# A layer 1 gate step whose operations are put in another order

## The chip, the cores and the metric

One core of a Trainium2 chip runs the whole program. Its engines are TensorE (PE; its weight loads are shown as PEld), VectorE (DVE), ScalarE (ACT), GpSimd (POOL) and SyncE (SP, which here issues transfers). Each engine takes its own instructions in the order in which the program issues them and waits where an instruction needs another engine's result. The metric is the time of one execution on the device in microseconds, as a median of several runs. The kernel before takes 1412.36 us (three runs, 1409.13 to 1415.45).

## The reference

The reference is an attention with pooled queries, followed by two feed-forward layers:

```python
q_pool = q.reshape(B, H, S // 2, 2, D).mean(axis=3)          # 4, 8, 576, 64
attn   = softmax(q_pool @ k^T / sqrt(D))                     # k: 4, 8, 1152, 64
x      = (attn @ v).transpose(0, 2, 1, 3).reshape(2304, 512)
h = x @ w1_in;  g = h - tanh(h);              x = g @ w1_out # 512 -> 2048 -> 512
h = x @ w2_in;  g = h * sigmoid(1.702 * h);   x = g @ w2_out # 512 -> 2048 -> 512
```

The weights arrive as 64-bit floats, the rest as 32-bit floats.

## The kernel before, in words

To keep accuracy, every operand of a matmul is held as a high part (rounded to the format that TensorE multiplies) and a low part (what the rounding left), and three products are added up: high by high, high by low, low by high. A high part is a copy on ScalarE; a low part is a subtraction, `value - high`, on GpSimd or VectorE with both inputs in SBUF.

The attention comes first and isn't touched. The two feed-forward layers are in `moe`. Tokens are cut into 6 blocks of 384 (`b`), the hidden width of 2048 into 4 quarters of 512 (`qq`), and each quarter into two halves (`fp`). A step is one (layer, quarter, block, half): steps 0 to 47 are layer 1, steps 48 to 95 layer 2, and 12 steps make a quarter. In step w TensorE computes h of step w (L552, 24 matmuls into one of two PSUM buffers) and then y of step w-2 (L627, 24 matmuls in layer 1), which lies in four PSUM banks. Even steps begin a sum in these banks and odd steps end it, so in odd steps the four banks are added to `xb` in SBUF (L640 on VectorE; in a layer's first quarter L638, a copy on ScalarE), and the even step behind begins its sum in a bank when the bank has been read.

`gate` makes g from h. In layer 1 that is a polynomial where |h| is small, and h - tanh(h) elsewhere. On ScalarE: u = h squared (L577), a and e, squares of u plus a constant (L580, L589), d = tanh(h) (L587), and a mask from u, written over a (L594). On VectorE: g = GC * u * h (L581), which reads h in PSUM; g = (a + GA1) * g (L584); d = h - d (L592), which reads h in PSUM; g = (e + GB1) * g (L595); and a predicated copy of d into g under the mask (L598). u, a, e and d have one buffer each, g has two. `split_g` of the step before stands in this step: the high part is L562 on ScalarE, the low part L564 on GpSimd in layer 1.

Weights of the next quarter are loaded and converted in eight pieces a quarter. A piece is a load (L109, two buffers), a first conversion step s0 (L122 on ScalarE; L123 and L127 on VectorE), a second one s1 (L134 and L138 on VectorE), and the split into high (L145, ScalarE) and low part (L146, GpSimd). A table gives for each of them a slot; there are two slots a step, one ahead of it and one behind it, so before the change these jobs never stand inside `gate`. The low parts of x for the next blocks or the next layer (L102, VectorE) are put into such slots too.

The order on every engine is the order of the program text (`tc.manual_schedule`); semaphores are added where one engine needs another.

Of the kernel before, what the change touches and what calls it, by code (L numbers as in the profile page):

```python
# [10 lines left out]
AF = mybir.ActivationFunctionType  # L11
ALU = mybir.AluOpType
# [6 lines left out]
GC = 0.006269319676  # L19
GA0, GA1 = 0.64716092, 2.51604723 ** 2  # L20
# [3 lines left out]
def f32(ap):  # L24
    return ap.bitcast(F32)
# [3 lines left out]
def tile_pooled_attention_two_moe(  # L29
# [11 lines left out]
    nc = tc.nc  # L41
# [9 lines left out]
    NB = NT // TB  # L51
    NKC = DM // 128
    DFF = w1_in.shape[0] * 128
    NQ = DFF // 512
# [43 lines left out]
    def split_x(b, cs, eng):  # L98
        for c in cs:
            hi, lo = xs[b][0][c], xs[b][1][c]  # L100
            nc.scalar.activation(hi, xb[b][:, c], AF.Copy)
            eng.tensor_tensor(lo, xb[b][:, c], f32(hi), op=ALU.subtract)  # L102
# [53 lines left out]
    def weight(kind, n):  # L156
        return slots[kind][n % NSLOT[kind]]
# [369 lines left out]
    def moe(ctx: ExitStack, ending):  # L527
        mp = ctx.enter_context(tc.tile_pool(name="moe", bufs=1))
        ps_h = ctx.enter_context(tc.tile_pool(name="ps_h", bufs=2, space=PSUM))
        ps_y = ctx.enter_context(tc.tile_pool(name="ps_y", bufs=4, space=PSUM))  # L530
        add_slot("o", mp.tile([128, 2 * DM], F32R, name="w3"))
        for b in range(1, NB):
            t = mp.tile([128, 2, NKC, TB], F32R, name=f"hl{b}")
            xs[b] = [[t[:, r, c] for c in range(NKC)] for r in range(2)]

        jobs = [(li, qq, b) for li in range(2) for qq in range(NQ) for b in range(NB)]
        steps = [(*j, fp) for j in jobs for fp in range(2)]
        gg, gs, yt = {}, {}, {}

        def temp(nm, bufs=1):  # L540
            return mp.tile([128, 2, TB], F32, tag=nm, name=nm, bufs=bufs)

        def h_part(n):
            li, qq, b, fp = steps[n]
            x = xs[b]
            hb = ps_h.tile([128, 2, 512], F32, tag="h", name="h")
            for j in range(2):
                wi = weight("i", li * NQ * 4 + qq * 4 + 2 * fp + j)
                k = 0
                for c in range(NKC):  # L550
                    for w, r in ((0, 0), (0, 1), (1, 0)):
                        nc.tensor.matmul(  # L552
                            hb[:, j, 0:TB], wi[:, c, w, :], x[r][c],
                            start=(k == 0), stop=(k == 3 * NKC - 1))
                        k += 1
            return hb[:, :, 0:TB]

        def split_g(n):
            li = steps[n][0]
            gt = mp.tile([128, 2, 2, TB], F32R, tag="g", name="g", bufs=3)  # L560
            g = gg.pop(n)
            nc.scalar.activation(gt[:, :, 0, :], g, AF.Copy)  # L562
            eng = nc.gpsimd if li == 0 else nc.vector
            eng.tensor_tensor(gt[:, :, 1, :], g, f32(gt[:, :, 0, :]), op=ALU.subtract)  # L564
            gs[n] = gt

        def gate(n, h, adds):

            g = temp("gg", 2)

            def add(scalar=False):
                if adds and adds[0][0] is scalar:
                    adds.pop(0)[1]()

            if steps[n][0] == 0:
                u, a, e, d = temp("u"), temp("a"), temp("e"), temp("d")
                nc.scalar.activation(u, h, AF.Square)  # L577
                if n > 0:
                    split_g(n - 1)
                nc.scalar.activation(a, u, AF.Square, bias=GA0)  # L580
                nc.vector.scalar_tensor_tensor(  # L581
                    out=g, in0=u, scalar=GC, in1=h, op0=ALU.mult, op1=ALU.mult)
                add()
                nc.vector.scalar_tensor_tensor(  # L584
                    out=g, in0=a, scalar=GA1, in1=g, op0=ALU.add, op1=ALU.mult)
                add(True)
                nc.scalar.activation(d, h, AF.Tanh)  # L587
                add(True)
                nc.scalar.activation(e, u, AF.Square, bias=GB0)  # L589
                add(True)  # L590
                add()
                nc.vector.tensor_sub(d, h, d)  # L592
                add()
                nc.scalar.activation(a, u, AF.Relu, bias=-T2)  # L594
                nc.vector.scalar_tensor_tensor(  # L595
                    out=g, in0=e, scalar=GB1, in1=g, op0=ALU.add, op1=ALU.mult)
                add()
                nc.vector.copy_predicated(g, a[:].bitcast(I32), d)  # L598
            else:
                split_g(n - 1)  # L600
                s = temp("a")
                nc.scalar.activation(s, h, AF.Sigmoid, scale=1.702)  # L602
                add()
                nc.vector.tensor_mul(g, h, s)
            gg[n] = g
            while adds:
                adds.pop(0)[1]()

        def y_part(n):
            li, qq, b, fp = steps[n]  # L610
            g = gs.pop(n)
            base = li * NQ * 4 + qq * 4 + 2 * fp
            nm, w = (NKC, TB) if li == 0 else (NTT, DM)
            if fp == 0:
                yt[li, qq, b] = [
                    ps_y.tile([128, 512], F32, tag="y", name="y") for _ in range(nm)]
            ys = yt[li, qq, b]
            for m in range(nm):
                k = 0
                for j in range(2):  # L620
                    wo = weight("o", base + j)
                    for p, r in ((0, 0), (0, 1), (1, 0)):
                        if li == 0:
                            lhsT, rhs = wo[:, p, m * 128:(m + 1) * 128], g[:, j, r, :]
                        else:
                            lhsT, rhs = g[:, j, p, m * 128:(m + 1) * 128], wo[:, r, :]
                        nc.tensor.matmul(  # L627
                            ys[m][:, 0:w], lhsT, rhs,
                            start=(fp == 0 and k == 0), stop=(fp == 1 and k == 5))
                        k += 1  # L630
            if fp == 0:
                return []
            acc = flat(xb[b])

            def add(m):
                dst = acc[:, m * w:(m + 1) * w]
                if qq == 0:
                    nc.scalar.activation(dst, ys[m][:, 0:w], AF.Copy)  # L638
                else:
                    nc.vector.tensor_add(dst, dst, ys[m][:, 0:w])  # L640
                if li == 1 and qq == NQ - 1:
                    r0 = b * TB + m * 128
                    nc.sync.dma_start(out=out[r0:r0 + 128, :], in_=dst)

            return [(qq == 0, lambda m=m: add(m)) for m in range(nm)]

        later = {}

        def at(slot, job):
            later.setdefault(slot, []).append(job)  # L650

        for slot, job in zip((2, 4, 8, 1, 1, 3), ending):
            at(slot, job)
        per = 4 * NB
        for qn in range(1, 2 * NQ):
            for kind, f, *when in (
# [3 lines left out]
            ):  # L660
                for job, o in zip(piece(kind, qn * 4 + f), when):
                    at((qn - 1) * per + o, job)
        for b in range(1, NB):
            for c in range(NKC):
                at(4 * b - 6 + c if b > 1 else 0, lambda b=b, c=c: split_x(b, [c], nc.vector))
        for b in range(NB):
            for c in range(NKC):
                at(NQ * per - 14 + 4 * b + 2 * c, lambda b=b, c=c: split_x(b, [c], nc.vector))

        for w in range(len(steps) + YLAG):  # L670
            if w == len(steps):
                split_g(w - 1)
            for go in later.pop(2 * w, ()):
                go()
            h = h_part(w) if w < len(steps) else None
            adds = y_part(w - YLAG) if w >= YLAG else []
            if h is not None:
                gate(w, h, adds)
            while adds:
                adds.pop(0)[1]()  # L680
            for go in later.pop(2 * w + 1, ()):
                go()
        assert not later

    with tc.manual_schedule():
        with ExitStack() as c1:
            ending = attention(c1)
# [46 lines left out]
```

## Time and profile before

| | before |
|---|---|
| median of 3 runs | 1412.36 us |
| profiled execution | 1410.96 us |
| its span, first to last instruction | 1409.2 us |
| mean granted TensorE clock | 0.983 |
| busy share of the span: PE, PEld, DVE, ACT, POOL | 94%, 88%, 78%, 60%, 32% |
| layer 1's first L581 to its last | 558.6 to 997.4 us |

The profile's times count from the span's first instruction. A row of a group of instructions has the line, the engine, the operation, the tiles (output, then inputs) with their shapes, the count, the busy time and the mean length of one, then the engine's idle time just before them and which engine and line ended most of it. A row of a timeline has the start, the length and the same names; what stands in brackets is the idle time before it and what ended that. Records of neighbouring instructions on one engine can overlap by about 0.1 us, since one is still writing when the next begins.

### The profile page before, as it was taken

To read this page: it belongs to the slowest core of one execution; us is meant where nothing else is said; L and a number is where in the kernel's file an instruction comes from. 1 tells how busy PE (TensorE), PEld (TensorE's weight loads), DVE (VectorE), ACT (ScalarE), POOL (GpSimd) and SP (SyncE) were. 2 spreads that over 40 slices of the span, in tenths; PEclk is the share of its full clock that TensorE was granted. 3 is DMA by queue.
4 is the path that set the end of the run, shared out by engine and by line. 5 is a ranking of instruction groups with operands and counts; after the bars stand their busy time and mean duration, and the time that the engine had idled before them with its cause. 6 is when DMAs were issued, how large, how long until landed. Compare 5 with 4: busy or idle time off the path is not lost.

```text
span 1409.2 us, 20874 instructions
## 1 busy us (share of the span) xinstructions
PE 1319.7 (94%) x7632; PEld 1246.7 (88%) x7632; DVE 1097.9 (78%) x1230; ACT 842.4 (60%) x1885; POOL 446.2 (32%) x314
## 2 busy tenths in 40 slices
PE   4999999999999888989999999988999999999998
PEld 3999989998989887889988988988999999999997
DVE  5888888889898978999999999999963454554433
ACT  2788888888888776676655555655643332222211
POOL 6344445444545435333332332332210110110000
PEclk9999999999999999999999999999999999999999
DMA  7576666575656542110111111111011110110011
GB/s 192 131 172 162 172 143 148 140 178 144 164 144 180 116 112 64 48 36 31 45 46 30 40 36 45 31 45 46 31 46 45 45 46 30 45 46 30 24 45 67
DMA packets 44039, 117.72 MB, mean 84 GB/s; under 512 B 11936, under 2 KB 11936, under 8 KB 43936
## 3 DMA queue, kind: packets, MB, share of 16 engines
q1 hardware_dynamic: 43900, 116.38, 31.3%
q8 instruction: 60, 0.98, 0.3%
q14 instruction: 43, 0.35, 0.1%
q10 hardware_dynamic: 36, 0.00, 0.0%
HBM read 66.58 MB, written 4.79 MB: 51 GB/s over the span
## 4 chain that ended last, share of the span: by engine, by line
PE 51%; DVE 25%; issue 8%; ACT 8%; DMA 4%; POOL 3%; SPq 2%; DVEq 0%; POOLq 0%; ACTq 0%
PE y L627 17%; PE h L552 16%; PE pv L348 9%; DVE wt L134 4%; PE mx L281 4%; DVE gg L584 3%; PE sc L319 3%; PE sc L320 3%; DVE gg L595 3%; DVE gg L598 2%; DVE gg L581 2%; DVE mt L284 2%; DVE wt L127 2%; ACT ph L323 2%; ACT pf L321 1%
## 5 line engine op out<-in xcount | busy, mean ns | idle before, releaser
L321 ACT ACTIVATE pf<-sc 128x288 f32<-128x288 f32 x576 | 244.6, 426 | 70.5 <-PE sc L320 67.1
L323 ACT ACTIVATE ph<-sc 128x288 fp32r<-128x288 f32 x564 | 243.8, 432 | 0.0
L284 DVE TENSOR_REDUCE mt<-mx 128x1 fp32r<-128x1152 f32 x144 | 194.0, 1349 | 55.7 <-PE mx L281 55.7
L332 DVE TENSOR_TENSOR pl<-pf,ph 128x576 fp32r<-128x576 f32 x224 | 208.4, 952 | 6.9 <-ACT ph L323 6.4
L319 PE MATMUL sc<-q,a 128*128 128x288 f32 x576 | 169.3, 305 | 10.2 <-ACT ph L323 4.1
L320 PE MATMUL sc<-q,a 65*128 65x288 f32 x576 | 167.1, 302 | 2.0 <-DMA q<-tt 2.0
L602 ACT ACTIVATE a<-h 128x768 f32<-128x768 f32 x48 | 39.0, 813 | 208.1 <-PE h L552 208.1
L640 DVE TENSOR_TENSOR xb<-xb,y 128x384 f32<-128x384 f32 (+1 forms) x126 | 76.0, 605 | 95.1 <-PE y L627 95.1
L348 PE MATMUL pv<-pl,vh 128*128 128x288 f32 x576 | 139.5, 306 | 10.6 <-POOL pl L332 7.1
L564 POOL TENSOR_TENSOR g<-gg,g 128x768 fp32r<-128x768 f32 x48 | 93.5, 1947 | 171.6 <-ACT g L562 168.5
L552 PE MATMUL h<-hl,w 128*128 128x384 f32 x720 | 134.1, 341 | 7.4 <-DVE hl L102 7.4
L348 PE MATMUL pv<-ph,vh 128*128 128x288 f32 x576 | 136.9, 301 | 3.9 <-ACT u L354 3.8
L552 PEld LDWEIGHTS h<-hl,w 128*128 128x128 f32 x720 | 128.8, 192 | 9.2 <-DVE hl L102 8.0
L562 ACT ACTIVATE g<-gg 128x768 fp32r<-128x768 f32 x96 | 81.2, 846 | 90.8 <-DVE gg L598 51.4
L348 PE MATMUL pv<-ph,vl 128*128 128x288 f32 x576 | 135.1, 298 | 0.0
L281 PE MATMUL mx<-kh,bdq 128*128 128x384 f32 x432 | 108.4, 362 | 26.2 <-DVE mt L284 18.7
L319 PEld LDWEIGHTS sc<-q,a 128*128 128x128 f32 x576 | 112.1, 195 | 17.6 <-ACT ph L323 11.1
L332 POOL TENSOR_TENSOR pl<-pf,ph 128x576 fp32r<-128x576 f32 x64 | 106.7, 1668 | 62.3 <-ACT ph L323 53.6
L320 PEld LDWEIGHTS sc<-q,a 65*128 65x128 f32 x576 | 111.4, 193 | 2.3 <-issue 2.2
L348 PEld LDWEIGHTS pv<-pl,vh 128*128 128x128 f32 x576 | 96.9, 191 | 16.2 <-POOL pl L332 9.4
L552 PE MATMUL h<-hl,bdq 128*128 128x384 f32 x600 | 108.4, 335 | 1.2 <-DVE d L592 1.2
L348 PEld LDWEIGHTS pv<-ph,vh 128*128 128x128 f32 x576 | 102.6, 192 | 6.8 <-ACT u L354 6.6
(114 smaller groups left out, 2910.1 us busy)
## 6 DMA issues: line engine op xcount, KB each, us to landing
a<-kh SPq DMA_DIRECT2D x64, 288.0 KB
raw<-in_moe_w_in_dram SPq DMA_DIRECT2D x32, 512.0 KB
raw<-in_moe_w_out_dram SPq DMA_DIRECT2D x32, 512.0 KB
qr<-in_q_dram SPq DMA_DIRECT2D x16, 576.0 KB
kr<-in_k_dram SPq DMA_DIRECT2D x16, 576.0 KB
vr<-in_v_dram SPq DMA_DIRECT2D x16, 576.0 KB
q<-qh SPq DMA_DIRECT2D x64, 144.0 KB
a<-kl SPq DMA_DIRECT2D x32, 288.0 KB
```

The source lines that it names most:

```text
L281: nc.tensor.matmul(mx[:, a, 0:384], bdqs[p % 2][:, j, :], d["kh"][:, a * 384:(a + 1) * 384], start=True, stop=True)
L284: nc.vector.tensor_reduce(d["mt"][:, j:j + 1], mx[:, :, 0:384], AX.XY, ALU.max, negate=True)
L319: nc.tensor.matmul(sc, a1[:, ks], q2[:, xs], start=True, stop=False)
L320: nc.tensor.matmul(sc, a2[:, ks], q3[:, xs], start=False, stop=True)
L321: nc.scalar.activation(pf[:, xs], sc, AF.Exp, scale=SCALE)
L323: nc.scalar.activation(ph[:, xs], sc, AF.Exp, scale=SCALE)
L332: eng.tensor_tensor(pl, pf, f32(ph[:]), op=ALU.subtract)
L348: nc.tensor.matmul(accs[hd][x], w[:, t, :], r[:, x * HB:(x + 1) * HB], start=(t == 0 and n == 0), stop=(t == KT - 1 and n == 2))
L552: nc.tensor.matmul(hb[:, j, 0:TB], wi[:, c, w, :], x[r][c], start=(k == 0), stop=(k == 3 * NKC - 1))
L562: nc.scalar.activation(gt[:, :, 0, :], g, AF.Copy)
L564: eng.tensor_tensor(gt[:, :, 1, :], g, f32(gt[:, :, 0, :]), op=ALU.subtract)
L627: nc.tensor.matmul(ys[m][:, 0:w], lhsT, rhs, start=(fp == 0 and k == 0), stop=(fp == 1 and k == 5))
```

## The change

In layer 1's `gate`, Tanh is issued right behind Square, and VectorE's L581 behind both; the split of the step before comes next, then one addition of y, the subtraction h - d, the other additions, and only then the operations on a, e and g and the predicated copy. The weights' jobs are no longer put into slots ahead of and behind a step but at named places: "split" and "convert" inside `gate`, "start" and "end" around the step. Both conversion steps of a piece now stand at one "convert" place, and the table of steps is new. The splits of x and the last jobs of the attention's end move to such places as well. What is computed stays the same.

```diff
--- before.py
+++ after.py
@@ -564,6 +564,15 @@
             eng.tensor_tensor(gt[:, :, 1, :], g, f32(gt[:, :, 0, :]), op=ALU.subtract)
             gs[n] = gt
 
+        later = {}
+
+        def at(w, place, job):
+            later.setdefault((w, place), []).append(job)
+
+        def run(w, place):
+            for go in later.pop((w, place), ()):
+                go()
+
         def gate(n, h, adds):
 
             g = temp("gg", 2)
@@ -575,33 +584,36 @@
             if steps[n][0] == 0:
                 u, a, e, d = temp("u"), temp("a"), temp("e"), temp("d")
                 nc.scalar.activation(u, h, AF.Square)
+                nc.scalar.activation(d, h, AF.Tanh)
+                nc.vector.scalar_tensor_tensor(
+                    out=g, in0=u, scalar=GC, in1=h, op0=ALU.mult, op1=ALU.mult)
                 if n > 0:
                     split_g(n - 1)
+                run(n, "split")
+                add()
+                nc.vector.tensor_sub(d, h, d)
+                add()
+                add()
+                add()
+                run(n, "convert")
                 nc.scalar.activation(a, u, AF.Square, bias=GA0)
-                nc.vector.scalar_tensor_tensor(
-                    out=g, in0=u, scalar=GC, in1=h, op0=ALU.mult, op1=ALU.mult)
-                add()
-                nc.vector.scalar_tensor_tensor(
-                    out=g, in0=a, scalar=GA1, in1=g, op0=ALU.add, op1=ALU.mult)
-                add(True)
-                nc.scalar.activation(d, h, AF.Tanh)
                 add(True)
                 nc.scalar.activation(e, u, AF.Square, bias=GB0)
                 add(True)
-                add()
-                nc.vector.tensor_sub(d, h, d)
-                add()
+                nc.vector.scalar_tensor_tensor(
+                    out=g, in0=a, scalar=GA1, in1=g, op0=ALU.add, op1=ALU.mult)
                 nc.scalar.activation(a, u, AF.Relu, bias=-T2)
                 nc.vector.scalar_tensor_tensor(
                     out=g, in0=e, scalar=GB1, in1=g, op0=ALU.add, op1=ALU.mult)
-                add()
                 nc.vector.copy_predicated(g, a[:].bitcast(I32), d)
             else:
                 split_g(n - 1)
                 s = temp("a")
                 nc.scalar.activation(s, h, AF.Sigmoid, scale=1.702)
+                run(n, "split")
                 add()
                 nc.vector.tensor_mul(g, h, s)
+                run(n, "convert")
             gg[n] = g
             while adds:
                 adds.pop(0)[1]()
@@ -644,42 +656,38 @@
 
             return [(qq == 0, lambda m=m: add(m)) for m in range(nm)]
 
-        later = {}
-
-        def at(slot, job):
-            later.setdefault(slot, []).append(job)
-
-        for slot, job in zip((2, 4, 8, 1, 1, 3), ending):
-            at(slot, job)
-        per = 4 * NB
+        for (w, place), job in zip(
+                ((0, "end"), (1, "end"), (3, "end"), (0, "convert"), (0, "convert"), (1, "split")),
+                ending):
+            at(w, place, job)
+        places = ("end", "convert", "convert", "split")
         for qn in range(1, 2 * NQ):
             for kind, f, *when in (
-                ("i", 0, 1, 5, 5, 7), ("o", 1, 3, 7, 8, 9), ("i", 1, 5, 9, 9, 11),
-                ("o", 0, 8, 13, 13, 15), ("i", 2, 10, 15, 16, 21), ("i", 3, 13, 17, 17, 23),
-                ("o", 2, 17, 23, 24, 25), ("o", 3, 19, 25, 27, 29),
+                ("i", 0, 0, 2, 2, 3), ("o", 1, 1, 3, 3, 5), ("i", 1, 2, 4, 4, 5),
+                ("o", 0, 3, 6, 6, 7), ("i", 2, 4, 8, 8, 11), ("i", 3, 6, 10, 10, 11),
+                ("o", 2, 8, 12, 12, 13), ("o", 3, 10, 13, 13, 14),
             ):
-                for job, o in zip(piece(kind, qn * 4 + f), when):
-                    at((qn - 1) * per + o, job)
-        for b in range(1, NB):
-            for c in range(NKC):
-                at(4 * b - 6 + c if b > 1 else 0, lambda b=b, c=c: split_x(b, [c], nc.vector))
+                for job, w, place in zip(piece(kind, qn * 4 + f), when, places):
+                    at((qn - 1) * 2 * NB + w, place, job)
         for b in range(NB):
             for c in range(NKC):
-                at(NQ * per - 14 + 4 * b + 2 * c, lambda b=b, c=c: split_x(b, [c], nc.vector))
+                if b > 0:
+                    at(max(0, 2 * b - 4 + c // 2), "end" if b > 1 else "start",
+                       lambda b=b, c=c: split_x(b, [c], nc.vector))
+                at(NQ * 2 * NB - 7 + 2 * b + c, "end",
+                   lambda b=b, c=c: split_x(b, [c], nc.vector))
 
         for w in range(len(steps) + YLAG):
             if w == len(steps):
                 split_g(w - 1)
-            for go in later.pop(2 * w, ()):
-                go()
+            run(w, "start")
             h = h_part(w) if w < len(steps) else None
             adds = y_part(w - YLAG) if w >= YLAG else []
             if h is not None:
                 gate(w, h, adds)
             while adds:
                 adds.pop(0)[1]()
-            for go in later.pop(2 * w + 1, ()):
-                go()
+            run(w, "end")
         assert not later
 
     with tc.manual_schedule():
```

## Rows read from the trace of the kernel before

**Rows 1.** Busy time by stretch: us, then PE, PEld, DVE, ACT, POOL, clock, DMA.

```profile
558.61:671.04 112.43, 101.70 (x548) 100.09 (x548) 105.97 (x113) 77.30 (x124) 37.56 (x19) 0.94 0.12 36
...
782.67:894.38 111.71, 104.78 (x578) 100.83 (x577) 107.22 (x118) 63.79 (x88) 36.12 (x20) 0.98 0.12 38
...
1010.00:1409.20 399.20, 395.39 (x1998) 359.44 (x1996) 197.21 (x265) 119.55 (x174) 33.75 (x26) 1.00 0.14 44
```

**Rows 2.** Chain that ended last, 645 to 690: start, length, what.

```profile
662.85 4.16 PE h L552 x24
667.01 4.16 PE y L627 x24
```

**Rows 3.** Waits of PE, 553 to 1010: total us, times, longest.

```profile
PE y L627 <- DVE xb L640: 20.1, 13, 3.5
```

**Rows 4.** Groups on DVE, 782.7 to 894.3: count, busy us, mean ns, idle.

```profile
L134 DVE SCALAR_TENSOR_TENSOR wt<-wa,wt 128x512 f32<-128x512 f32 x8 | 16.5, 2061 | 0.7
L584 DVE SCALAR_TENSOR_TENSOR gg<-a,gg 128x768 f32<-128x768 f32 x12 | 15.4, 1285 | 2.6 <-ACT a L580 2.2
L595 DVE SCALAR_TENSOR_TENSOR gg<-e,gg 128x768 f32<-128x768 f32 x12 | 15.3, 1278 | 0.0
L598 DVE COPY_PREDICATED gg<-a,d 128x768 f32<-128x768 int32 x12 | 14.7, 1222 | 0.6
...
L127 DVE SCALAR_TENSOR_TENSOR wt<-raw,wt 128x512 int32<-128x512 int32 x8 | 7.5, 938 | 0.3
```

**Rows 5.** Timeline, 861 to 870: start, length, instruction.

```profile
861.54 0.95 DVE L595 SCALAR_TENSOR_TENSOR gg<-e,gg 128x768 f32<-128x768 f32 x1
...
862.47 0.80 ACT L577 ACTIVATE u<-h 128x768 f32<-128x768 f32 x1
862.59 1.08 DVE L598 COPY_PREDICATED gg<-a,d 128x768 f32<-128x768 int32 x1
...
863.56 0.41 DVE L123 TENSOR_SCALAR wt<-raw 128x512 int32<-128x512 int32 x1
863.76 0.85 ACT L562 ACTIVATE g<-gg 128x768 fp32r<-128x768 f32 x1 [0.50 <-DVE gg L598]
864.00 0.69 DVE L127 SCALAR_TENSOR_TENSOR wt<-raw,wt 128x512 int32<-128x512 int32 x1
...
864.69 1.84 POOL L564 TENSOR_TENSOR g<-gg,g 128x768 fp32r<-128x768 f32 x1 [7.14 <-ACT g L562]
864.80 2.28 DVE L134 SCALAR_TENSOR_TENSOR wt<-wa,wt 128x512 f32<-128x512 f32 x1
...
867.72 0.95 DVE L581 SCALAR_TENSOR_TENSOR gg<-u,h 128x768 f32<-128x768 f32 x1
...
868.59 0.55 DVE L640 TENSOR_TENSOR xb<-xb,y 128x384 f32<-128x384 f32 x1
868.71 0.81 ACT L587 ACTIVATE d<-h 128x768 f32<-128x768 f32 x1 [3.36 <-DVE gg L581]
869.05 0.95 DVE L584 SCALAR_TENSOR_TENSOR gg<-a,gg 128x768 f32<-128x768 f32 x1
869.41 0.84 ACT L589 ACTIVATE e<-u 128x768 f32<-128x768 f32 x1
```

**Rows 6.** Line L592: count, ns shortest/median/longest, first and last start.

```profile
L592 DVE TENSOR_TENSOR d<-h,d x48: 943/951/955, 560.5 to 1000.6; 128x768 f32<-128x768 f32 x48
```

**Rows 7.** Line L587: what ended ScalarE's idle time before it, us, times.

```profile
  DVE gg L581: 105.5, 34
```

**Rows 8.** Timeline, layer 2, 1020 to 1023.

```profile
1020.82 1.30 POOL L146 TENSOR_TENSOR vh<-wt,vh 128x512 fp32r<-128x512 f32 x1 [9.30 <-ACT vh L145]
1021.13 1.27 DVE L123 TENSOR_SCALAR wt<-raw 128x512 int32<-128x512 int32 x1
```

**Rows 9.** Groups on DVE, 558.7 to 671.0.

```profile
L102 DVE TENSOR_TENSOR hl<-xb,hl 128x384 fp32r<-128x384 f32 x16 | 10.8, 702 | 0.2 <-ACT hl L101 0.2
```

**Rows 10.** Chain that ended last, 979 to 1010.

```profile
984.21 5.99 PE y L627 x24
```

## The prediction

> **What bounds the kernel now.** I read the page's forty slices first (behind the attention VectorE is nearly full and TensorE just under it, then the other way round), then the busy time by stage. In two quarters of layer 1 VectorE is busy 94 and 96% and TensorE 90 and 94%; in layer 2 TensorE is busy 99% and VectorE 49% [rows 1]. So a change to the layer 1 step can move layer 1 only. Layer 1 has 48 steps; the windows are cut where the first VectorE operation of steps 0, 12, 24 and 36 begins (L581), so twelve steps take 112.4, 111.6 (from 671.04 to 782.67, the gap between two windows) and 111.7 us, 9.3 us a step. In the few stretches where TensorE works without a pause, a block of 24 matmuls of h or of y takes 4.16 us [rows 2]: 8.32 us a step, 99.8 us for twelve. TensorE's longest waits in layer 1 are for VectorE's additions of y [rows 3]. VectorE's queue therefore sets the pace and TensorE is the floor under it, 12 us a quarter lower.
>
> Why VectorE takes 9.3 us: in the third quarter, taking 0.69 us as the undisturbed length of the conversion's L127 and L134, 0.95 of L584 and L595 and 1.07 of L598, the five means give 8x1.37 + 8x0.25 + 12x0.335 + 12x0.33 + 12x0.15 = 22.7 us of lengthening [rows 4]. The cause is in the timeline: GpSimd's low part (L564) runs from 864.69 to 866.53; L134, begun at 864.80, ends at 867.08, 0.55 after GpSimd [rows 5]. An operation that reads PSUM never shows this: L592 is 943 to 955 ns in all 48 steps [rows 6]. So operations with two SBUF inputs stand still while GpSimd reads, and PSUM readers don't; that is what the change plays on. If all 22.7 us went, VectorE's queue would need 89 us a quarter and TensorE would be the bound.
>
> **The change, part by part.** (a) *Tanh moves ahead of VectorE's first operation.* Today Tanh (L587) waits for L581 in 34 of the 48 steps, 105.5 us in all [rows 7], though both only read h: at 868.71 Tanh begins 0.04 us after L581's end, while h had been there for over 6 us (Square had begun to read it at 862.47) [rows 5]. Readers of one h on two engines take turns in program order. After the change Tanh is issued first, so L581 waits for Tanh. And Tanh writes d, of which there is one buffer, read last by the copy_predicated (L598) of the step before. So a new chain stands in each step: L598's end, 0.09 to ScalarE (863.67 to 863.76), Tanh 0.81, 0.04 back: 0.94 us in which VectorE has nothing queued that may run (conversions, which filled this place, now stand later in the step). Against today's pitch, where the next operation starts 0.11 us before L598's recorded end (862.59 + 1.08 to 863.56), it costs 1.05 us a step, 12.6 us a quarter. Square isn't in the chain: it comes after Relu and ends before L598 does.
>
> The Trainium skill, "PSUM — Partial Sum Buffer", section "PSUM bank collisions raise a hardware error", says that ScalarE and VectorE may not touch one bank at once, reads included, and that a dependency is put between such instructions. The trace agrees (0.04 us behind L581). By this rule a quarter comes out as below; without it the gap would be gone and TensorE's 99.8 us would hold.
>
> (b) *What is left of the port stalls.* I count a step from L598's end to the next L598's end. L581 starts at 0.94. The copy g (L562, 0.85) follows Tanh at ScalarE's pitch of 0.70, from 0.79 to 1.64; GpSimd starts 0.08 later (864.61 to 864.69): low part from 1.72 to 3.56. A weight's low part (L146, 1.30 [rows 8]) queues behind it, to 4.88, a second one later still.
>
> Even step with a conversion: L581 0.94, L592 1.81 (pitch 0.87, as L581 to L640 [rows 5]), then the conversion's L123 at 2.68. Does a tensor_scalar with one SBUF input stand still? In layer 2 it did: begun at 1021.13 under L146, it took 1.27 us and ended 0.28 after it [rows 8]. So L123 ends at 3.84 in place of 3.09, 0.75 lost. The conversion needs 2.57 (863.56 to 867.72 less L134's 1.59 of stall), so L584 starts at 6.0, L595 at 7.05 and L598 at 8.1 (an operation that needs the one before follows 1.05 later, 861.54 to 862.59 [rows 5]), end 9.16.
>
> Odd step with y's additions: 0.94, addition 1.81, L592 2.27, additions at 3.14, 3.60, 4.06 (0.46 apart, 868.59 to 869.05), L584 4.52, L595 5.57, L598 6.62, end 7.7. Here GpSimd is hidden to 4.52; one L146 sticks out by 0.2 (7.9). With two, L584 and L595 each lose a turn: 8.9. Odd with conversion and one L146: 7.7 + 2.57 + 0.2 = 10.5. Even with conversion and L146: 9.16 + 1.1 = 10.3.
>
> The new table gives, in a quarter, five even conversion steps, one of 10.3, two of 10.5 (offsets 1 and 3: two of the eight conversions do fall into steps with additions), two of 8.9, one of 7.9, one of 7.7: 45.8 + 10.3 + 21.0 + 17.8 + 7.9 + 7.7 = **110.5 us**, against 111.6 and 111.7. Check from the other side: 111.7 - 22.7 + 12.6 + 8.7 (stalls left: 3.75 + 1.9 + 0.66 + 2.4) + 2.2 (six odd steps whose last three operations now follow one another directly) - 2.2 (L584's waits for ScalarE's a [rows 4], which go) = 110.3. The stalls fall by 14 us and the Tanh gap takes 12.6 of them.
>
> (c) *First quarter.* Additions are on ScalarE. In an odd step L584 is then ready at 2.68 and ends some 0.8 behind GpSimd at 4.4 (0.55 for 512 elements [rows 5], so about 0.8 for 768: an estimate), and Relu, behind ScalarE's additions, lets L598 begin near 6.1: 7.2, with one L146 7.6 to 7.9, with two 8.6. Sixteen low parts of x (L102, today 10.8 us on VectorE [rows 9]) now come two at the ends of steps 0 to 7 and 0.47 us each run just in the Tanh gap, at no cost; if that cover were gone, 7.5 us. Steps 0 to 11: 8.2 (0.7 for Tanh and a conversion step without a low part, 7.5), 7.6, 9.2, 10.3, 9.2, 8.6, 9.2, 7.9, 9.2, 7.2, 9.2, 8.6, and an estimated 1.5 for the normalisation behind steps 0 and 3: 105.9 against 112.4, -6.5.
>
> (d) *Last quarter.* Steps 36 to 44 are 110.5 less 7.7, 9.2 and 8.9 = 84.7; y of step 44 then starts 1.56 later (L581, addition, start), at 86.3. Today it starts at 984.21 [rows 10], 89.8 after 894.38: -3.5, because the low parts of x for layer 2 also fall into gaps. That block takes 5.99 us as its four banks come free one by one; the earlier additions let it run at about 4.16, less 0.4 for its successor's wait: -1.4. From there TensorE runs without a pause today.
>
> (e) *At nothing.* Loads: a raw buffer comes free earlier in a step and is wanted earlier in a later one, by about as much; SP's queue holds only these loads there, so nothing waits behind one. Layer 2's moved conversions: VectorE is half idle [rows 1]; if they delayed an addition by their 2.57 us, TensorE has a 4.16 us block of h in between. y of step w waits for its low part at 3.56 in step w+1 and is done 4.16 later, 5.5 us before the last addition of step w+2 wants it, so TensorE isn't late anywhere.
>
> Sum: -6.5 - 1.2 - 1.2 - 3.5 - 1.4 = -13.8 us on the profiled execution's 1410.96 (span 1409.2): 1397. That run is 1.4 under the median 1412.36; I forecast **1399**.
>
> **Bounds.** The gap's price: nothing if the turns aren't taken, 12.6 + 9.6 us a quarter if Square (0.80) came into it because h is late. I take 12.6, for all its parts have rows. Stalls left: from 0 to today's 22.7; I take 8.7, the count by the new table.
>
> **Rivals.** 1. *No gap:* Tanh of a step is free to run beside L598. A quarter of VectorE is then 97.9, TensorE's 99.8 bounds, and 45 steps at 8.32 reach y of step 44 some 47 us earlier: 1364. Against it: 34 turns taken, and one d. 7%.
> 2. *The stalls stay* (slower): in even steps only 0.96 of GpSimd's 1.84 us lies beside PSUM readers; if GpSimd is later than 1.72, or takes the port back between the five conversion operations, each L564 and L146 again blocks one operation, on top of the gap. It decides from 8.7 + 13.8/3.75 = 12.4 us of stalls a quarter; with all of today's the time is 1450, halfway (15.7) 1423. For it: L127 and L134 lose 13 us a quarter today; against it: half of the conversions then meet no L146. 15%.
> 3. *A wash:* gap 0.2 to 0.35 us longer by semaphores or a late Square, 9 to 16 us in 45 steps: 1406 to 1413. 23%. The forecast has 55%; its own range is 1385 to 1405.
>
> 0.5% (7 us) is about what a measurement of this kernel can tell from no change. Faster beyond it: 0.61; within: 0.23; slower: 0.16. The range 1382 to 1420 leaves out most of rival 1 and the far part of rival 2.
>
> **What would show it.** (a) VectorE idle about 0.9 us before each L581, released by Tanh, and Tanh released by L598; if L581 follows L598 directly, (a) is wrong. (b) L584, L595 and L598 at their undisturbed 0.95 and 1.07, L134 at 0.69, and L123 near 1.2 in even steps; stalls near 9 us a quarter. Quarters near 106, 110.5, 110.5. The forecast is wrong if the gap is absent, or if L127 and L134 keep means over 0.9.

## The result, and the profile after

The changed kernel takes 1396.32 us (median of 4 runs, 1390.82 to 1398.61) against 1413.24 us for the kernel before in the same comparison (4 runs, 1409.13 to 1415.45): ratio 0.988, 95% interval 0.984 to 0.992. The forecast was 1399. The profiled execution took 1398.61 us, its span 1396.8 us against 1409.2.

Busy time by stretch of the kernel after, cut like [rows 1] at the first VectorE operation of steps 0, 12, 24 and 36 (columns as there):

```profile
562.08:665.66 103.58, 98.63 (x547) 96.55 (x547) 94.36 (x109) 75.20 (x122) 33.68 (x18) 0.97 0.14 44
665.66:775.18 109.52, 105.15 (x586) 102.52 (x585) 94.42 (x113) 66.17 (x93) 34.11 (x20) 0.98 0.13 39
775.18:884.84 109.66, 103.62 (x578) 99.50 (x577) 94.56 (x116) 64.77 (x89) 33.85 (x20) 1.00 0.12 39
```

The quarters took 112.4, 111.6 and 111.7 us and now take 103.6, 109.5 and 109.7. VectorE is busy 86% of the third quarter, where it was 96%, and yet the quarter is only 2 us shorter. The timeline at the beginning of step 24, an even step with a conversion, shows why (ScalarE's and GpSimd's rows stand between VectorE's; TensorE's are left out):

```profile
773.15 1.09 DVE L608 COPY_PREDICATED gg<-a,d 128x768 f32<-128x768 int32 x1
774.27 0.81 ACT L587 ACTIVATE d<-h 128x768 f32<-128x768 f32 x1 [1.46 <-DVE gg L608]
774.98 0.84 ACT L562 ACTIVATE g<-gg 128x768 fp32r<-128x768 f32 x1
775.18 0.95 DVE L588 SCALAR_TENSOR_TENSOR gg<-u,h 128x768 f32<-128x768 f32 x1 [0.94 <-ACT d L587]
...
775.89 1.86 POOL L564 TENSOR_TENSOR g<-gg,g 128x768 fp32r<-128x768 f32 x1 [3.66 <-ACT g L562]
776.05 0.95 DVE L594 TENSOR_TENSOR d<-h,d 128x768 f32<-128x768 f32 x1
...
776.91 1.12 DVE L123 TENSOR_SCALAR wt<-raw 128x512 int32<-128x512 int32 x1
...
778.07 0.69 DVE L127 SCALAR_TENSOR_TENSOR wt<-raw,wt 128x512 int32<-128x512 int32 x1
778.87 0.69 DVE L134 SCALAR_TENSOR_TENSOR wt<-wa,wt 128x512 f32<-128x512 f32 x1
...
782.32 1.08 DVE L608 COPY_PREDICATED gg<-a,d 128x768 f32<-128x768 int32 x1
```

(L588 is the first operation, before L581; L594 the subtraction, before L592; L603, L606 and L608 were L584, L595 and L598; the additions are L652.) Tanh begins 0.03 us after the predicated copy ends, the first operation 0.10 after Tanh, and VectorE stands idle for 0.94 us. GpSimd's low part, 775.89 to 777.75, runs beside the subtraction, which reads h in PSUM, at no cost; L123 meets its end and takes 1.12 in place of 0.41; L134, which took 2.28 beside GpSimd in [rows 5], takes 0.69. From copy end to copy end the step takes 9.16 us (774.24 to 783.40).

VectorE's groups over the third quarter, answering to [rows 4] (count, busy us, mean ns, idle time before):

```profile
L606 DVE SCALAR_TENSOR_TENSOR gg<-e,gg 128x768 f32<-128x768 f32 x12 | 13.3, 1110 | 1.3
L608 DVE COPY_PREDICATED gg<-a,d 128x768 f32<-128x768 int32 x12 | 12.9, 1077 | 1.2
...
L603 DVE SCALAR_TENSOR_TENSOR gg<-a,gg 128x768 f32<-128x768 f32 x12 | 11.7, 975 | 0.0
L588 DVE SCALAR_TENSOR_TENSOR gg<-u,h 128x768 f32<-128x768 f32 x12 | 11.4, 954 | 11.2 <-ACT d L587 11.2
...
L123 DVE TENSOR_SCALAR wt<-raw 128x512 int32<-128x512 int32 x8 | 7.7, 964 | 0.0
L127 DVE SCALAR_TENSOR_TENSOR wt<-raw,wt 128x512 int32<-128x512 int32 x8 | 6.5, 813 | 0.3
L134 DVE SCALAR_TENSOR_TENSOR wt<-wa,wt 128x512 f32<-128x512 f32 x8 | 5.5, 692 | 0.8
```

The lengthening is 8x0.55 (L123) + 8x0.12 (L127) + 12x0.15 (L606) + 0.4 (L603, L608) = 7.6 us, where it was 22.7. In exchange L588 has 11.2 us of idle time before it, all ended by Tanh. Over the whole layer it waits for Tanh in 34 of 48 steps; at the layer's beginning and end x's low parts (L102) fill the gap.

Where the 12.4 us of the two spans lie: the first h begins at 556.2 in place of 553.4, 2.8 later, in the attention, which the change doesn't touch (over the ten profiled kernels of this study, all with the same attention, the first VectorE operation of layer 1 starts anywhere from 555.1 to 565.1). From there to y of step 44 it is 415.3 us against 430.8, -15.5; to the first h of layer 2 -1.3; over layer 2's first quarter +1.7; the rest is equal.

### The profile page after: what moved, and what is told of

It reads as the page before. It is cut to its first block, busy times and chain, and to the rows that moved or that the text cites. A ratio compares the mean times of both kernels' runs of the same rounds, so it can differ in the third digit from the quotient of the medians.

```text
span 1396.8 us, 20802 instructions
## 1 busy us (share of the span) xinstructions
PE 1316.1 (94%) x7632; PEld 1243.2 (89%) x7632; DVE 1048.5 (75%) x1230; ACT 843.7 (60%) x1885; POOL 439.5 (31%) x314
## 4 chain that ended last, share of the span: by engine, by line
PE 47%; DVE 28%; ACT 9%; issue 5%; DMA 4%; POOL 3%; SPq 3%; DVEq 0%; POOLq 0%; ACTq 0%
PE y L639 14%; PE h L552 14%; PE pv L348 9%; PE mx L281 4%; DVE gg L606 3%; DVE gg L603 3%; PE sc L319 3%; DVE gg L608 3%; PE sc L320 3%; DVE d L594 3%; DMA vr<-in_v_dram 2%; ACT d L587 2%; DVE wt L123 2%; DVE wt L127 2%; DVE gg L588 2%
## 5 line engine op out<-in xcount | busy, mean ns | idle before, releaser
L564 POOL TENSOR_TENSOR g<-gg,g 128x768 fp32r<-128x768 f32 x48 | 89.0, 1853 | 300.3 <-ACT g L562 281.0
L652 DVE TENSOR_TENSOR xb<-xb,y 128x384 f32<-128x384 f32 (+1 forms) x126 | 73.0, 606 | 93.2 <-PE y L639 93.2
L281 PE MATMUL mx<-kh,bdq 128*128 128x384 f32 x432 | 108.4, 362 | 24.4 <-DVE mt L284 16.8
L552 PE MATMUL h<-hl,w 128*128 128x384 f32 x720 | 130.5, 335 | 0.0
L605 ACT ACTIVATE a<-u 128x768 f32<-128x768 f32 x48 | 40.7, 848 | 131.8 <-DVE gg L603 131.8
L320 PEld LDWEIGHTS sc<-q,a 65*128 65x128 f32 x576 | 111.6, 194 | 3.1 <-issue 3.1
L615 DVE TENSOR_TENSOR gg<-h,a 128x768 f32<-128x768 f32 x48 | 45.8, 955 | 84.8 <-ACT a L612 84.8
L348 PEld LDWEIGHTS pv<-ph,vh 128*128 128x128 f32 x576 | 102.5, 192 | 7.1 <-ACT u L354 6.9
```

The source lines that it names most:

```text
L281: nc.tensor.matmul(mx[:, a, 0:384], bdqs[p % 2][:, j, :], d["kh"][:, a * 384:(a + 1) * 384], start=True, stop=True)
L320: nc.tensor.matmul(sc, a2[:, ks], q3[:, xs], start=False, stop=True)
L348: nc.tensor.matmul(accs[hd][x], w[:, t, :], r[:, x * HB:(x + 1) * HB], start=(t == 0 and n == 0), stop=(t == KT - 1 and n == 2))
L552: nc.tensor.matmul(hb[:, j, 0:TB], wi[:, c, w, :], x[r][c], start=(k == 0), stop=(k == 3 * NKC - 1))
```

## The experiments

My theory: the change takes 14 us of stalls behind GpSimd out of a quarter and puts a Tanh gap of 12.6 us in. Against it stood that the gap isn't what it seems, that the stalls fall for other reasons, and that the order and the new places don't share the gain as I thought. Every time below is a median, each ratio is against the kernel before in the same comparison.

**1. Take the gap away by d's buffer.** d and e take turns in two shared buffers, so that Tanh needn't wait for the copy.

```diff
-                u, a, e, d = temp("u"), temp("a"), temp("e"), temp("d")
+                u, a = temp("u"), temp("a")
+                first, second = temp("de", 2), temp("de", 2)
+                d, e = (first, second) if n % 2 == 0 else (second, first)
```

> The changed kernel with one edit: d and e share two buffers and change places every step, so Tanh of a step writes where e of the step before lay, and waits for that step's L606 (g = (e + GB1) * g) and no more for its predicated copy. Theory (the gap of 0.94 us before each first VectorE operation is the chain copy, Tanh, first operation through the one buffer of d): Tanh then starts when Square is done, about 0.6 us before the copy's end; the gap shrinks to about 0.25 us, an even step with a conversion from 9.16 to about 8.5 us, a quarter from 109.6 to about 101.3 us; with TensorE's floor of 99.8 near, 1365 to 1375 us. Rival (the first operation is late for another reason, h's arrival or Square's): gap and time stay, 1396 us. Second rival (the stalls come back as GpSimd's low part falls on other operations): gap gone, the mean of the conversion's operations up by 0.6 us each, time 1385 to 1396 us.

Measured: 1373.25 us, ratio 0.974 (0.971 to 0.977). The second and third quarters take 102.5 and 102.2 us. VectorE's rows around the start of step 34, then ScalarE's, then a group of the third quarter:

```profile
848.12 1.08 DVE L610 COPY_PREDICATED gg<-a,de 128x768 f32<-128x768 int32 x1
849.47 0.95 DVE L590 SCALAR_TENSOR_TENSOR gg<-u,h 128x768 f32<-128x768 f32 x1 [0.27 <-ACT de L589]
```

```profile
847.87 0.81 ACT L588 ACTIVATE u<-h 128x768 f32<-128x768 f32 x1
848.58 0.81 ACT L589 ACTIVATE de<-h 128x768 f32<-128x768 f32 x1
```

```profile
L123 DVE TENSOR_SCALAR wt<-raw 128x512 int32<-128x512 int32 x8 | 8.8, 1101 | 0.0
```

Tanh (here L589) now follows Square directly and ends 0.19 us behind the copy; the gap is 0.27 us. It is the chain through d that cost the changed kernel some 20 us (0.014 of the ratio; 23 between medians of two comparisons). This version beats both kernels; with that of experiment 2, from which the ratios don't tell it apart, it is the fastest found that computes the whole.

**2. Take the gap away by the turns.** d keeps one buffer; Tanh goes back behind the first operation and the subtraction behind the additions.

```diff
-                nc.scalar.activation(d, h, AF.Tanh)
                 nc.vector.scalar_tensor_tensor(
                     out=g, in0=u, scalar=GC, in1=h, op0=ALU.mult, op1=ALU.mult)
                 if n > 0:
                     split_g(n - 1)
+                nc.scalar.activation(d, h, AF.Tanh)
                 run(n, "split")
                 add()
-                nc.vector.tensor_sub(d, h, d)
                 add()
                 add()
                 add()
+                nc.vector.tensor_sub(d, h, d)
```

> The changed kernel with Tanh issued behind VectorE's first operation (as before the change) and the subtraction h - d behind all four additions; d keeps its one buffer. Theory (the gap needs Tanh's turn on h ahead of the first operation as well as d's one buffer, so taking either away ends it): the first operation follows the predicated copy at once, Tanh runs beside the additions in odd steps; in even steps the subtraction waits for Tanh until about 1.75 us behind the copy, which puts the conversion's L123 near GpSimd's end and leaves it 0.1 us of stall in place of 0.75; an even step with a conversion 8.5 us, a plain odd step 6.7 us, a quarter about 101.5 us; 1368 to 1378 us. Rival (the 0.94 us only move from ahead of the first operation to ahead of the subtraction): a quarter 108 us or more, 1388 to 1396 us.

Measured: 1377.35 us, ratio 0.972 (0.969 to 0.975); a quarter takes 101.8 us, an even step with a conversion 8.5, the plain odd one 6.67. VectorE's groups in the third quarter:

```profile
L597 DVE TENSOR_TENSOR d<-h,d 128x768 f32<-128x768 f32 x12 | 11.5, 958 | 5.3 <-ACT d L591 5.3
L587 DVE SCALAR_TENSOR_TENSOR gg<-u,h 128x768 f32<-128x768 f32 x12 | 11.3, 943 | 0.0
```

The wait for Tanh has moved ahead of the subtraction but is 5.3 us a quarter and no longer 11.2: 0.88 us in each of the six even steps, none in the odd ones, where the additions cover it. So the gap before the first operation needs both: Tanh's turn on h first, and d's one buffer.

**3. Take the port stalls away.** In the kernel before, and in the changed one, GpSimd's low part of g in layer 1 is left out: a memset writes zeros to the same tile and reads nothing.

```diff
-            eng.tensor_tensor(gt[:, :, 1, :], g, f32(gt[:, :, 0, :]), op=ALU.subtract)
+            if li == 0:
+                nc.gpsimd.memset(f32(gt[:, :, 1, :]), 0.0)
+            else:
+                eng.tensor_tensor(gt[:, :, 1, :], g, f32(gt[:, :, 0, :]), op=ALU.subtract)
```

For the kernel before:

> The kernel before, in which GpSimd's low part of g in layer 1 (L564) is a memset to zero: the low part of g is left out, so the output lacks it; GpSimd still writes the tile but reads nothing. Theory (two-input VectorE operations stand still because GpSimd reads SBUF): L134, L584 and L595 fall to 0.69 and 0.95 us but for the weights' low parts, the lengthening from 22.7 to about 6 us a quarter, and TensorE bounds: 1365 to 1380 us. Rival (they stand still for something else at that place, such as ScalarE's copy into the same tile or a semaphore): the means stay, 1410 us.

For the changed kernel:

> The changed kernel, in which GpSimd's low part of g in layer 1 (L564) is a memset to zero: the low part of g is left out. Theory (of the stalls left in a quarter, 7.6 us by the trace, all but those behind the weights' low parts fall, while the Tanh gap of 0.94 us stays in every step): a quarter 103 to 105 us, 1370 to 1380 us, and VectorE still idle about 0.9 us before each first operation. Rival (the gap is itself due to GpSimd): the gap goes too, TensorE bounds at 99.8 us, 1358 us as the kernel before with the same edit.

Measured: the kernel before falls to 1358.08 us (0.963, 0.960 to 0.967), below the 1365 to 1380 that I expected, and its third quarter takes 99.8 us, in which TensorE is busy throughout (columns as in [rows 1]):

```profile
754.60:854.40 99.80, 99.80 (x577) 99.80 (x576) 92.92 (x117) 62.98 (x89) 21.78 (x20) 1.00 0.13 43
```

The changed kernel falls to 1371.1 us only (0.971, 0.969 to 0.973), with 103.5 us a quarter. VectorE's groups, third quarter, first of the former:

```profile
L587 DVE SCALAR_TENSOR_TENSOR gg<-a,gg 128x768 f32<-128x768 f32 x12 | 11.5, 957 | 2.3 <-ACT a L583 1.9
...
L134 DVE SCALAR_TENSOR_TENSOR wt<-wa,wt 128x512 f32<-128x512 f32 x8 | 5.5, 690 | 0.7
```

and of the latter:

```profile
L591 DVE SCALAR_TENSOR_TENSOR gg<-u,h 128x768 f32<-128x768 f32 x12 | 11.5, 954 | 10.6 <-ACT d L590 10.6
...
L123 DVE TENSOR_SCALAR wt<-raw 128x512 int32<-128x512 int32 x8 | 4.9, 619 | 0.0
```

L134's mean goes from 2061 to 690 ns and L584's (here L587) from 1285 to 957 once GpSimd reads nothing there. That alone doesn't prove it, since the memset needn't wait for ScalarE and mostly runs elsewhere in the step. Rows that do lie beside a memset settle it: in layer 1 of the changed kernel eight L609 (L595 before the change) begin while one runs, and each takes its undisturbed 0.96 us. So for operations with two SBUF inputs the stalls are due to GpSimd's reads; L123 is another matter (last section). The stalls behind the weights' low parts stay in both kernels. The Tanh gap stays (10.6 us), so it isn't GpSimd's. With the reads of g gone the kernel before is the faster of the two, by 13 us between the medians of two comparisons (0.963 against 0.971).

**4. The order alone, and the places alone.** First the kernel before with the new order of `gate` and the old slots:

```diff
                 nc.scalar.activation(u, h, AF.Square)
+                nc.scalar.activation(d, h, AF.Tanh)
+                nc.vector.scalar_tensor_tensor(
+                    out=g, in0=u, scalar=GC, in1=h, op0=ALU.mult, op1=ALU.mult)
                 if n > 0:
                     split_g(n - 1)
...
```

> The kernel before with the order of gate alone changed (Tanh and the first operation first, then the split, the subtraction, additions, and the rest); conversions and splits keep their slots ahead of and behind the steps. Theory (the order brings the gain, the new places give half of it back because they leave the Tanh gap empty): conversions in their slots fill the gap; a quarter 100 to 104 us, 1363 to 1382 us, faster than the whole change's 1396 us. Rival (the gain comes from keeping the conversions off GpSimd's low parts of weights, that is from the new places): 1396 to 1413 us, and the stalls of L127 and L134 as before the change, near 13 us a quarter.

Measured: 1406.89 us, ratio 0.998 (0.996 to 1.000). My theory was wrong here. VectorE's groups of its third quarter:

```profile
L134 DVE SCALAR_TENSOR_TENSOR wt<-wa,wt 128x512 f32<-128x512 f32 x8 | 13.2, 1648 | 0.7
...
L579 DVE SCALAR_TENSOR_TENSOR gg<-u,h 128x768 f32<-128x768 f32 x12 | 11.4, 947 | 2.8 <-ACT d L578 2.8
L127 DVE SCALAR_TENSOR_TENSOR wt<-raw,wt 128x512 int32<-128x512 int32 x8 | 11.3, 1419 | 0.3
L138 DVE SCALAR_TENSOR_TENSOR wt<-raw,wt 128x512 int32<-128x512 int32 x9 | 9.3, 1030 | 0.3
```

The conversions do fill the gap (2.8 us of it left), but there L127, L134 and L138 meet GpSimd's low parts, of weights and of g, and lose 5.8 + 7.7 + 3.0 = 16.5 us a quarter, more than the 13 us of before the change. With the operations on g that is some 18 us of lengthening against 22.7, and the 2.8 us of gap take most of the difference.

Then the changed kernel with the old order of `gate`, the split place behind the split of g and the convert place behind the subtraction (shown against the order before the change):

```diff
                 if n > 0:
                     split_g(n - 1)
+                run(n, "split")
                 nc.scalar.activation(a, u, AF.Square, bias=GA0)
...
                 nc.vector.tensor_sub(d, h, d)
                 add()
+                run(n, "convert")
                 nc.scalar.activation(a, u, AF.Relu, bias=-T2)
```

> The changed kernel with the old order of gate: first operation, then a and L584's turn, Tanh behind the first operation, the subtraction, then the new convert place, then the rest; the new split place stands behind the split of g. Theory by the durations of the trace (no Tanh gap, as Tanh follows the first operation; but L584 now meets GpSimd's low part of g in every step and loses 1.1 to 1.9 us, while the conversions run free behind it): an even step with a conversion 9.2 us, plain odd steps 7.8 us, a quarter about 107 us; 1385 to 1393 us, that is the new places bring all of the gain and the order none. Rival (the order of VectorE's operations is what gains): 1405 us or above, near the order's own -3 us away from before.

Measured: 1389.93 us, ratio 0.985 (0.983 to 0.986), not to be told apart from the whole change's 0.988 (0.984 to 0.992). The theory held in the time. The price stands in VectorE's groups again:

```profile
L594 DVE SCALAR_TENSOR_TENSOR gg<-a,gg 128x768 f32<-128x768 f32 x12 | 19.6, 1632 | 11.9 <-ACT a L590 11.9
```

L584 (here L594) waits 11.9 us a quarter for a and stands still 8.1 us behind GpSimd; the conversions run free (L134 at 692 ns). In a step that is 1.67 us, within the 1.1 to 1.9 of the expectation, but the larger part is a wait for ScalarE, which the expectation didn't name. So the new places bring the gain. The new order trades L584's wait and stall for Tanh's gap and L123's stall, about one for one.

**5. Fill the gap with conversions.** Both conversion steps of a piece stand behind the step before that of their convert place.

```diff
-        places = ("end", "convert", "convert", "split")
+        places = ("end", "end", "end", "split")
...
-                for job, w, place in zip(piece(kind, qn * 4 + f), when, places):
-                    at((qn - 1) * 2 * NB + w, place, job)
+                for j, (job, w, place) in enumerate(zip(piece(kind, qn * 4 + f), when, places)):
+                    at((qn - 1) * 2 * NB + w - (j in (1, 2)), place, job)
```

> The changed kernel with one edit: both conversion steps of a piece stand behind the step before the one whose convert place they had, so that VectorE runs them between a predicated copy and the next first operation. Theory (VectorE is idle there and the conversion's tensor_scalar stands still 0.75 us behind GpSimd only because it comes at 2.68 us): the 2.57 us of a conversion fill the gap, the next first operation starts at about 2.5 in place of 0.94 us, L123's stall is gone; an even step takes about 7.3 us in place of 9.16, a quarter 97 to 101 us with TensorE's 99.8 as the floor; 1360 to 1370 us. Rival (conversions must stand in steps without additions, after the subtraction, or GpSimd's low parts block them again): L127 to L138 grow to means of 1.2 us and more, time 1396 us or above.

Measured: 1392.09 us, ratio 0.987 (0.985 to 0.990), a third quarter of 108.5 us: a miss by over 20 us. The timeline shows what the expectation had left out:

```profile
806.40 1.08 DVE L608 COPY_PREDICATED gg<-a,d 128x768 f32<-128x768 int32 x1
...
809.14 1.87 POOL L564 TENSOR_TENSOR g<-gg,g 128x768 fp32r<-128x768 f32 x1 [7.24 <-ACT g L562]
809.34 2.22 DVE L138 SCALAR_TENSOR_TENSOR wt<-raw,wt 128x512 int32<-128x512 int32 x1
```

and the group that it is so in the whole quarter (each of them takes 2.21 to 2.23 us):

```profile
L138 DVE SCALAR_TENSOR_TENSOR wt<-raw,wt 128x512 int32<-128x512 int32 x9 | 20.0, 2222 | 0.3
```

GpSimd started 1.66 us behind the copy, L138 at 1.86, and every conversion lost 1.53 us for 0.2 us. The expectation asked only what becomes of L123; by the 1.72 us at which the prediction itself had GpSimd begin, the last operation of the conversion came too late as well. The gap was filled (3.7 us of idle time left in the quarter), L123's stall was gone, and one new stall took nearly all of it.

**6. Push L123 past GpSimd, on top of experiment 1.** Two of the four additions go to the end of the step, behind the copy.

```diff
                 nc.vector.tensor_sub(d, h, d)
                 add()
-                add()
-                add()
                 run(n, "convert")
```

> The kernel in which d and e share two buffers, with two of the four additions of y left to the end of the odd step, behind the predicated copy, where they read PSUM while GpSimd makes the low part of the next step. Theory (VectorE's queue still bounds at 102.2 us a quarter, 4.3 us of it L123's stall): the additions fill the remaining gap of 0.27 us and push L123 behind GpSimd's end, a quarter 99.8 to 101 us, 1364 to 1370 us. Rival (TensorE is near its floor, so late additions hold its block of y and whatever VectorE saves is lost there): 1373 to 1385 us, with TensorE waiting for L654.

Measured: 1388.09 us, ratio 0.983 (0.982 to 0.985), 3 us above the rival's range; what the rival named did come. TensorE's longest waits in layer 1, here and then in experiment 1:

```profile
PE y L639 <- DVE xb L652: 12.3, 6, 4.4
```

```profile
PE y L641 <- POOL g L564: 4.5, 6, 1.5
...
PE y L641 <- DVE xb L654: 1.1, 1, 1.1
```

VectorE's own idle time grows too, before its first operations from 2.7 us in the third quarter of experiment 1 to 4.8. One of TensorE's waits, of 2.29 us, from 807 on, is followed by a stretch in which the granted clock is 0.55, most of it at the lower of the two levels (1.2 of 2.4 GHz), and nine matmuls are 2.66 us busy, where nine had been 1.40 at 1.00 before it:

```profile
805.60:807.00 1.40, 1.40 (x9) 1.13 (x7) 1.30 (x3) 0.31 (x1) 0.00 (x0) 1.00 0.31 41
809.30:812.00 2.70, 2.66 (x9) 2.66 (x10) 2.70 (x4) 2.54 (x4) 1.84 (x1) 0.55 0.00 0
```

## Why the prediction was right

**The bound: right.** With the stalls behind the low parts of g gone and no gap the kernel before takes 99.8 us for a quarter, with TensorE busy throughout, which is the floor that [rows 2] gave: VectorE's queue bounds layer 1, and TensorE stands 12 us under it.

**(a) The Tanh gap: right in cause and size.** 0.94 us was forecast and 0.94 is read in step 24, released by Tanh, which the copy had released; 11.2 us of idle time a quarter against 12.6 us of price (the price also counts the 0.11 us by which operations otherwise overlap). Experiments 1 and 2 break the chain at either of its two links, and with either the time falls by some 20 us, though in experiment 2 six waits of 0.88 us a quarter remain at another place. The Trainium skill, "PSUM — Partial Sum Buffer", section "PSUM bank collisions raise a hardware error", which asks for a dependency between readers of one bank on two engines, agrees with the runs: in none of the ten traces does a reader of an h begin before the other engine's reader of the same h has ended.

**(b) The stalls left: right, a little high.** 8.7 us a quarter were forecast, 7.6 measured; an even step with a conversion 9.16 and 9.16, the plain odd one 7.7 and 7.74 (start to start, step 33), the two with conversion and weights' low part 10.5 and 10.4. The third quarter came out at 109.7 against 110.5. In the steps with two weights' low parts L606 lost a whole turn and L603 hardly any (8.7 in place of 8.9). So the sign that L595 would be back at 0.95 us didn't come: its mean (L606) is 1110 ns. And that operations that read PSUM aren't held up was forecast from rows that show little of it: of the 48 subtractions of [rows 6] only one ran beside a low part of GpSimd. After the change 47 do, and now it is shown:

```profile
L594 DVE TENSOR_TENSOR d<-h,d x48: 937/951/952, 563.0 to 987.5; 128x768 f32<-128x768 f32 x48
```

**(c), (d) The first and last quarter.** Steps 0 to 11 took 103.6 us from the first operation, against 105.9 less 0.7 for the first Tanh (the plain odd step took 6.57 us where 7.2 was counted); L102's mean fell from 702 [rows 9] to 545 ns, as it now runs in the gap. Steps 36 to 44 took 84.45 against 84.7, and the stretch from y of step 44 to layer 2 is 1.3 shorter, against 1.4.

**(e) Costed at nothing: wrong by 1.7 us.** The step that failed, as the prediction put it: "if they delayed an addition by their 2.57 us, TensorE has a 4.16 us block of h in between". VectorE's rows in step 49 of the kernel after, and TensorE's wait:

```profile
1000.64 1.02 DVE L102 TENSOR_TENSOR hl<-xb,hl 128x384 fp32r<-128x384 f32 x2
1001.58 2.06 DVE L564 TENSOR_TENSOR g<-gg,g 128x768 fp32r<-128x768 f32 x1
1003.56 0.54 DVE L652 TENSOR_TENSOR xb<-xb,y 128x384 f32<-128x384 f32 x1
1004.02 0.94 DVE L615 TENSOR_TENSOR gg<-h,a 128x768 f32<-128x768 f32 x1
1004.89 0.41 DVE L123 TENSOR_SCALAR wt<-raw 128x512 int32<-128x512 int32 x1
...
1007.47 1.48 DVE L652 TENSOR_TENSOR xb<-xb,y 128x384 f32<-128x384 f32 x3
```

```profile
PE y L639 <- DVE xb L652: 1.1, 1, 1.1
```

At layer 2's beginning x's low parts and a low part of g on VectorE already make the first addition late; the conversion, now between the additions, comes on top, and TensorE waits 1.1 us for the second. Layer 2's first quarter takes 101.3 us against 99.7. No run took this alone away, so the cause is read, not shown. The other traces bear on it: with the old slots this quarter takes 99.7 us in all three (the kernel before and its variants in experiments 3 and 4), with the new places 100.4 to 101.7 in six of seven. The seventh, the changed kernel of experiment 3, has the conversion at the same place and takes 99.7, and there the second addition begins 21.1 us behind layer 2's first h, not 23.1. So the late conversion alone doesn't make the wait; VectorE has to come late to it as well. In experiment 5, where it stands elsewhere, the quarter is as long (101.3 us), with TensorE waiting 1.3 us for low parts of g and 0.4 for an addition.

**What the forecast didn't separate.** It gave the 14 us of stalls to the change as a whole. The runs divide them: the places alone bring the whole gain, the order alone 0.2 percent. My expectation for the order alone, 1363 to 1382 us, was wrong because I let the conversions fill the gap without asking what GpSimd does in it. **The rivals:** "no gap" is what experiment 1 nearly makes, at 1373 and not 1364, since 0.27 us of gap a step and 5.5 us of L123's stall a quarter (1101 ns against 416, eight times) stay; "the stalls stay" is largely what the order alone does.

The medians lie 16.9 us apart and the forecast said 13.8; in the two profiled executions layer 1 and its end gave 16.8, layer 2 took 1.7 back and the attention of that one execution 2.8. That those two executions differ by 12.4 us, so near the 13.8, is in part luck: layer 1 gave 3 us more than forecast (8.2 for 6.5 in the first quarter, 2.1 and 2.0 for 1.2 each in the next two), and layer 2 and the attention took 4.5 back. An attention that starts layer 1 some microseconds earlier or later from kernel to kernel is more than what is left of the difference.

## What to carry to other kernels

When an operation is moved ahead of another engine's, follow both what it reads in turns and which single buffer it writes: an operation that waits for the last reader of its only buffer, and is waited for by the first operation of the next step, makes a gap in every step that has nothing else to run there, and a second buffer or a place behind that first operation ends it. Where two engines hold each other up, place each operation by what the other does at that moment, with a margin: 0.2 us decided whether a conversion lost 1.53 us. And before trading one stall for another, try the parts of the change singly; here one part carried all of it.

## What the runs showed of the hardware that I had not expected

That L123, a tensor_scalar with one SBUF input, stands still behind GpSimd the prediction had read from one row of layer 2; in layer 1 it does so too (964 ns mean against 416 before the change), so not only operations with two SBUF inputs do. What I had not expected stands in the changed kernel of experiment 3, in which GpSimd's memset reads nothing:

```profile
791.35 1.42 POOL L565 MEMSET g<- 128x768 f32 x2
792.41 0.63 DVE L123 TENSOR_SCALAR wt<-raw 128x512 int32<-128x512 int32 x1
...
812.17 0.74 POOL L565 MEMSET g<- 128x768 f32 x1
812.48 0.96 DVE L609 SCALAR_TENSOR_TENSOR gg<-e,gg 128x768 f32<-128x768 f32 x1
```

L609, with two SBUF inputs, isn't held up. L123, begun beside a memset, is, and ends 0.28 us behind it, as in all three cases in layer 1 where it met a memset alone (0.63 to 0.65 us), and as it does behind GpSimd's low parts. The Trainium skill, "SBUF — State Buffer", section "Who interferes with whom", says that the port pair is an exclusive lock for the whole instruction and that tensor_scalar can take it in its two-port mode. The runs agree that L123 is held to the end of GpSimd's instruction, of one that only writes too; in which mode it ran no run shows. The same to-the-end stall is seen on L138 in experiment 5: begun 0.20 us behind GpSimd, it ended 0.55 us behind GpSimd's end, as L134 did in [rows 5], begun 0.11 behind it.
